# Attention with its row-maximum scores taken from the keys' high parts, two chunks at a time on two halves of TensorE's rows

## The chip, the cores and the metric

The kernel runs on one NeuronCore of a Trainium2 chip; the other cores are idle. The metric is the device time of one execution in microseconds. The engines have the profile's names: PE (TensorE's matmuls), PEld (its weight loads, which overlap with PE), DVE (VectorE), ACT (ScalarE), POOL (GpSimd) and SP (SyncE, which here only issues transfers). PSUM has eight banks of 2 KB for each of 128 partitions; a matmul writes to a bank, and DVE or ACT must read it before it can be used again.

## The reference

Attention for 4 batches and 12 heads of 448 tokens and 64 features, then two MLPs of 768 to 3072 to 768 features. All inputs and outputs are float32.

```python
def rmsnorm(x, g):
    rms = np.sqrt(np.mean(x * x, axis=-1, keepdims=True) + 1e-06)
    return x / rms * g
q_n, k_n = (rmsnorm(q, g_q), rmsnorm(k, g_k))
scores = scale * np.matmul(q_n, k_n.transpose(0, 1, 3, 2))
scores = scores - np.max(scores, axis=-1, keepdims=True)
attn = np.exp(scores)
attn = attn / (np.sum(attn, axis=-1, keepdims=True) + 1e-09)
return np.matmul(attn, v)
...
x = x + np.maximum(layernorm(x) @ w_ch1, 0.0) @ w_ch2
u = x + (token mixing of x by U and V, rank 32)
return u + np.maximum(u @ w_ch1, 0.0) @ w_ch2
```

The maximum that is subtracted appears in the numerator and in the sum under it. Another value near it gives the same quotient, apart from rounding.

## The kernel before

The kernel has two stages. Attention comes first, head by head, for 48 heads (up to about 345 us in the profile); the two MLPs follow, with an order of their own by a planner of costs and due times that the change does not touch. During attention some of the MLP weights are already loaded and prepared (`early`, `late`), and the layer norm of the batches that are done runs beside the heads (`ln_stats`, `ln_apply`).

Matrix products of float32 quality are made from float32r operands, which PE takes in one pass, with less precision. A value is split into a high part (its float32r rounding) and a low part (the rest). For each pair of heads `pre` makes from the raw inputs the token-wise tiles `qd` (the high part of q, written twice side by side), `kk` (high and low part of k side by side) and `ql` (the low part of q, and two columns more).

A head n then goes through these tasks, each written as a generator that is advanced once in each of the 4 steps of an iteration:

- `t1` (L419 to L437) turns `kk` and `qd` on PE so that features lie on partitions: `a1` [128, 448] has the high part of k on partitions 0 to 63 and the low part on 64 to 127, `bq` [128, 448] has the high part of q on both halves. ACT copies both from their banks (L427, L435).
- `mx` (L439 to L451) first copies the high part of k from `a1` into a second tile `a2` by a transfer on SP (L441). Then, for each of 4 chunks of 112 query tokens, one matmul (L445) gives the scores of the chunk with queries on partitions ("turned", since the later scores have keys there), and DVE takes each query's maximum from the bank (L446). ACT writes the negated maxima into a column of `ql` (L451).
- `t2` (L453 to L462) turns `ql`; its column with the maximum becomes a row that meets a row of ones in `a2`, so the later score matmul subtracts the maximum.
- `sc` (L464 to L486): for each of 4 chunks of 112 key tokens two matmuls into one bank, a 128-row one of `a1` and `bq` (L471) and a 66-row one of `a2` and the turned `ql` (L472); then ACT takes the exponential (L475).
- `pv` (L488 to L503): 4 products of exponentials and values (L496), float32, each issued as two instructions, accumulate in one bank `po`. The value tile `vf` has 128 columns: 64 of values, 64 filled with ones by POOL at the start (L260). So row 64 of `po` is the sum under the quotient.
- `norm` (L505 to L515): DVE copies rows 0 to 64 of `po` to `u` (two buffers), and SP stores them to `x` and to a table of sums (L513, L514).

The order around the change is written out by hand. `OS` is "smpabn": in iteration i the tasks are `sc` of head i, `mx` of head i + 2, `pv` of i - 1, `t1` of i + 3, `t2` of i + 1 and `norm` of i - 2, and each of the 4 steps advances each of them once in this order, after the background tasks (`pre`, `pre_v`). So PE gets in each step L471, L472, L445, L496, and at the end of the first three steps the turnings of k (L424), of `ql` (L459) and of q (L432). All engines run their instructions in order. The framework adds the waits, and lets the seven banks of this stage (`bank`, L61; an eighth serves the layer norm) go round among all these tasks.

Of the kernel before, what the change touches and what calls it, by code (L numbers as in the profile page):

```python
# [9 lines left out]
F32R = mybir.dt.float32r  # L10
# [4 lines left out]
ALU = mybir.AluOpType  # L15
AX = mybir.AxisListType

B, H, S, D = 4, 12, 448, 64
P = 128
CP = 112  # L20
NC = S // CP
# [14 lines left out]
QW = D + 2  # L36
# [7 lines left out]
def f32(ap):  # L44
    return ap.bitcast(F32)


def build(tc, qkv, gg, g_ln, w1a, w2a, w1b, w2b, u_in, v_in, out):
    nc = tc.nc
    V, A, PL, PE = nc.vector, nc.scalar, nc.gpsimd, nc.tensor  # L50
    with ExitStack() as es:
# [9 lines left out]
        def bank(name, tag=None):  # L61
            cnt[0] += 1
            tag = tag or banks["tag"]
            return banks["pool"].tile([P, 512], F32, tag=tag, name=f"{name}{cnt[0]}", bufs=banks[tag])
# [161 lines left out]
        def attention(ap, ep, ep2, early, late):  # L226
# [3 lines left out]
            st = {}  # L230
# [22 lines left out]
            for i in range(2):  # L253
                for lst, nm, dt, one in ((vfs, "vf", F32, 1.0), (vhs, "vh", F32R, 1.0), (vls, "vl", F32R, 0.0)):
                    n = NX if nm == "vf" else NC - NX
                    if n == 0:
                        lst.append(None)
                        continue
                    t = ap.tile([CP, 2, n, P], dt, tag=f"{nm}{i}", name=f"{nm}{i}")
                    PL.memset(f32(t[:, :, :, D:P]), one)  # L260
                    lst.append(t)
            for i in range(NA2):
                t = ap.tile([P, S], F32R, tag=f"a2{i}", name=f"a2{i}")
# [3 lines left out]
            for i in range(3):  # L267
                t = ep.tile([CP, 2 * NC, QW], F32R, tag=f"ql{i}", name=f"ql{i}")
# [150 lines left out]
            def t1(n):  # L419
                pr, j = divmod(n, 2)  # L420
                qd, ql, kk = st["tok", pr]
                pk = bank("pk")
                for c in range(NC):
                    PE.transpose(pk[:, c * CP:(c + 1) * CP].bitcast(F32R),  # L424
                                 kk[:, j * NC + c].rearrange("p a d -> p (a d)"), identr)
                a1 = ep2.tile([P, S], F32R, tag="a1", name=f"a1_{n}", bufs=T1 + 1)
                A.copy(a1, pk[:, :S])  # L427
                yield
                yield
                pq = bank("pq")  # L430
                for c in range(NC):
                    PE.transpose(pq[:, c * CP:(c + 1) * CP].bitcast(F32R),  # L432
                                 qd[:, j * NC + c].rearrange("p a d -> p (a d)"), identr)
                bq = ep2.tile([P, S], F32R, tag="bq", name=f"bq_{n}", bufs=T1 + 1)
                A.copy(bq, pq[:, :S])  # L435
                a2 = a2s[n % NA2]
                st["ab", n] = (a1, bq, a2)  # L437

            def mx(n):  # L439
                a1, bq, a2 = st["ab", n]  # L440
                nc.sync.dma_start(f32(a2[0:D, :]), f32(a1[0:D, :]))  # L441
                m = ap.tile([CP, NC], F32, tag="m", name=f"m{n}", bufs=2)
                for c in range(NC):
                    pm = bank("pm")
                    PE.matmul(pm[:CP, :S], bq[:, c * CP:(c + 1) * CP], a1, start=True, stop=True)  # L445
                    V.tensor_reduce(m[:, c:c + 1], pm[:CP, :S], AX.X, ALU.max)  # L446
                    if c < NC - 1:
                        yield
                pr, j = divmod(n, 2)
                ql = st["tok", pr][1]  # L450
                A.mul(ql[:, j * NC:(j + 1) * NC, D:D + 1], m.unsqueeze(2), -1.0)  # L451
# [36 lines left out]
            def pv(n):  # L488
                pr, j = divmod(n, 2)
                ps = st.pop(("p", n))  # L490
                vf, vh, vl = vfs[pr % 2], vhs[pr % 2], vls[pr % 2]
                po = bank("po")
                st["po", n] = po
                for c in range(NC):
                    if c < NX:
                        PE.matmul(po[:, :S], vf[:, j, c, :], ps[c], start=(c == 0), stop=(c == NC - 1))  # L496
                    else:
                        ph, pl = ps[c]
                        PE.matmul(po[:, :S], vh[:, j, c - NX, :], ph, start=(c == 0), stop=False)
                        PE.matmul(po[:, :S], vl[:, j, c - NX, :], ph, start=False, stop=False)  # L500
                        PE.matmul(po[:, :S], vh[:, j, c - NX, :], pl, start=False, stop=(c == NC - 1))
                    if c in PVY:
                        yield  # L503
# [55 lines left out]
            def ORD(i):  # L559
                fs = {"s": (sc, i), "m": (mx, i + MX), "p": (pv, i - 1), "a": (t1, i + T1), "b": (t2, i + T2), "n": (norm, i - NL)}  # L560
                return [fs[z] for z in OS]

            for i in range(-3 - T1, NH + 2):
                def ok(n):
                    return 0 <= n < NH
                if i == -3 - T1:
                    start = first_two()
# [40 lines left out]
        bufs, held, rings, ready = {}, {}, {}, {}  # L608
# [807 lines left out]
        with tc.tile_pool(name="raw", bufs=4) as rpool, tc.tile_pool(name="wf", bufs=3) as fpool:  # L1416
            with tc.tile_pool(name="ps", bufs=8, space=bass.MemoryType.PSUM) as psum:
                banks.update(pool=psum, tag="ps", ps=7, ln=1)
                with tc.tile_pool(name="att", bufs=1, side="right") as ap:
                    with tc.tile_pool(name="tok", bufs=1) as ep, tc.tile_pool(name="feat", bufs=1) as ep2:  # L1420
                        most, last = attention(ap, ep, ep2, early(), late())
# [70 lines left out]
```

## Time and profile before

| what | value |
|---|---|
| median of 3 runs (lowest to highest) | 1695.33 us (1694.02 to 1695.81) |
| profiled execution: span from its first to its last instruction | 1694.2 us |
| PE busy in the span | 1667.5 us (98%) |
| attention's matmuls | 11.6 to 345 us |
| the MLPs | from 345 us to the end |

Times in the rows further down are microseconds from the start of the span, unless they are marked as ns. A group of instructions has its line in the kernel, its engine, its operation, out <- in by the program's names, its shape and its count. A matmul's end is modelled and lies after the start of the next one, so durations of matmuls overlap; what one costs is read from the starts. A wait names the engine and line that ended it.

### The profile page before, as it was taken

The numbers are of one execution on the slowest core, as the hardware profiler recorded it, in microseconds if no ns is written. First come the engines' busy times: TensorE is split into PE (matmuls) and PEld (weight loads), VectorE is DVE, ScalarE is ACT, GpSimd is POOL, SyncE is SP. The second block draws the span as 40 slices with busy tenths as digits, with TensorE's granted clock in tenths as the row PEclk, the third lists the DMA queues.
The fourth block names the chain that finished last, engine by engine and source line by source line (L and its number), as shares of the span: only waits on it lengthen the run. The fifth ranks groups of instructions, "written<-read, shape, count | busy, mean of one in ns | idle before, by whom it ended". The sixth has DMA issues, their size and how long they took to land.

```text
span 1694.2 us, 24616 instructions
## 1 busy us (share of the span) xinstructions
PE 1667.5 (98%) x8223; PEld 1458.6 (86%) x8223; DVE 1198.0 (71%) x1913; ACT 997.2 (59%) x2098; POOL 1038.3 (61%) x924
## 2 busy tenths in 40 slices
PE   8999999999999999999999999999999999999999
PEld 6666666688898989999999999999999999999998
DVE  6767877878787876966767777666667864565665
ACT  6777878767777786554544455444445533544541
POOL 5445767457667777765555678545555645766752
PEclk8999999999999999999999999999999999999999
DMA  3434444775655576443544426565566563443442
GB/s 94 107 92 125 120 117 125 214 218 186 194 180 169 183 215 213 160 157 125 157 143 163 153 90 226 199 207 208 193 215 225 187 205 122 149 140 122 149 128 77
DMA packets 134430, 273.39 MB, mean 161 GB/s; under 512 B 37280, under 2 KB 57664, under 8 KB 134304
## 3 DMA queue, kind: packets, MB, share of 16 engines
q1 hardware_dynamic: 112252, 265.24, 49.4%
q10 hardware_dynamic: 22052, 6.59, 1.6%
q8 instruction: 65, 1.06, 0.3%
q14 instruction: 61, 0.50, 0.1%
HBM read 178.80 MB, written 81.96 MB: 154 GB/s over the span
## 4 chain that ended last, share of the span: by engine, by line
PE 85%; DVE 5%; DMA 4%; ACT 2%; issue 1%; POOL 1%; SPq 1%; DVEq 0%; ACTq 0%; POOLq 0%
PE bank L1104 31%; PE bank L1282 29%; PE po L496 6%; PE bank L1226 6%; PE b L1104 2%; PE ps L471 2%; PE pm L445 2%; PE b L1226 2%; PE ps L472 2%; DMA raw<-in_qkv 1%; DVE wf L83 1%; DMA r<-rs 1%; PE t L971 1%; PE xt L961 1%; PE pk L424 1%
## 5 line engine op out<-in xcount | busy, mean ns | idle before, releaser
L1282 PE MATMUL bank<-h,w 128*128 128x448 f32 x2655 | 588.6, 366 | 6.5 <-DVE x L1293 5.0
L1282 PEld LDWEIGHTS bank<-h,w 128*128 128x128 f32 x2655 | 497.0, 188 | 48.8 <-DVE x L1293 6.9
L1293 DVE TENSOR_TENSOR x<-x,bank 128x448 f32<-128x448 f32 x450 | 274.8, 615 | 182.1 <-PE bank L1282 177.8
L1104 PE MATMUL bank<-xh,w 128*128 128x448 f32 x1158 | 330.7, 367 | 0.0
L778 POOL TENSOR_TENSOR w<-wf,w 128x384 fp32r<-128x384 f32 x201 | 221.9, 1114 | 153.7 <-ACT w L777 143.8
L778 POOL TENSOR_TENSOR w<-s,w 128x384 fp32r<-128x384 f32 x151 | 171.8, 1141 | 161.5 <-ACT w L777 156.3
L1104 PE MATMUL bank<-T,w 128*128 128x448 f32 x1134 | 252.5, 367 | 2.9 <-DVE tm L1145 2.9
L1104 PEld LDWEIGHTS bank<-xh,w 128*128 128x128 f32 x1158 | 217.0, 188 | 18.3 <-issue 0.7
L1104 PEld LDWEIGHTS bank<-T,w 128*128 128x128 f32 x1134 | 211.7, 188 | 20.8 <-issue 2.7
L1104 PE MATMUL bank<-xl,w 128*128 128x448 f32 x579 | 211.9, 366 | 0.0
L777 ACT CAST w<-s 128x384 fp32r<-128x384 f32 x151 | 77.1, 514 | 171.9 <-PE bank L1104 164.0
L496 PE MATMUL po<-p,vf 112*128 112x448 f32 x384 | 176.1, 541 | 0.0
L777 ACT CAST w<-wf 128x384 fp32r<-128x384 f32 x201 | 102.4, 517 | 107.6 <-PE bank L1104 83.5
L446 DVE TENSOR_REDUCE m<-pm 112x1 f32<-112x448 f32 x192 | 118.5, 619 | 62.3 <-PE pm L445 61.6
L83 DVE SCALAR_TENSOR_TENSOR wf<-wf,raw 128x384 uint32<-128x384 uint32 x180 | 129.3, 724 | 23.0 <-ACT raw L75 10.1
L1104 PEld LDWEIGHTS bank<-xl,w 128*128 128x128 f32 x579 | 108.7, 188 | 8.9
L778 POOL TENSOR_TENSOR w<-raw,w 128x384 fp32r<-128x384 f32 x72 | 79.6, 1121 | 57.7 <-ACT w L777 57.7
L79 ACT ACTIVATE wf<-raw 128x384 f32<-128x384 f32 x180 | 99.4, 554 | 23.9 <-DMA raw<-in_w2a 14.5
L475 ACT ACTIVATE p<-ps 112x448 f32<-112x448 f32 x192 | 104.7, 546 | 3.2 <-PE pm L445 2.6
L71 ACT ACTIVATE raw<-raw 128x384 uint32<-128x384 uint8 x180 | 100.0, 557 | 0.0
L1096 DVE SCALAR_TENSOR_TENSOR h<-tm,h 128x448 fp32r<-128x448 f32 x103 | 97.1, 943 | 3.7 <-ACT h L1095 2.8
L471 PE MATMUL ps<-bq,a 128*112 128x448 f32 x192 | 98.7, 514 | 0.9 <-DVE m L446 0.9
(261 smaller groups left out, 2884.7 us busy)
## 6 DMA issues: line engine op xcount, KB each, us to landing
wd<-wf SPq DMA_DIRECT2D x94, 384.0 KB
ws<-w SPq DMA_DIRECT2D x84, 384.0 KB
w<-ws SPq DMA_DIRECT2D x84, 384.0 KB
wf<-wd SPq DMA_DIRECT2D x51, 384.0 KB
raw<-wd SPq DMA_DIRECT2D x48, 384.0 KB
raw<-in_w1b SPq DMA_DIRECT2D x48, 384.0 KB
raw<-in_w2b SPq DMA_DIRECT2D x48, 384.0 KB
raw<-in_w2a SPq DMA_DIRECT2D x44, 384.0 KB
```

Of the source, the lines that this page charges most:

```text
L71: A.activation(r[:, :, 0], r.bitcast(U8).rearrange("p n (t q) -> p n t q", t=2)[:, :, 0, 3], AF.Copy, scale=1.0 / 32, bias=-31.0 / 64)
L83: V.scalar_tensor_tensor(f, f, 3, r[:, :, 0], ALU.logical_shift_left, ALU.bitwise_or)
L446: V.tensor_reduce(m[:, c:c + 1], pm[:CP, :S], AX.X, ALU.max)
L471: PE.matmul(pb[:CP, :S], a1[:, cs], bq, start=True, stop=False)
L475: A.activation(p, pb[:CP, :S], AF.Exp)
L496: PE.matmul(po[:, :S], vf[:, j, c, :], ps[c], start=(c == 0), stop=(c == NC - 1))
L777: job(A, 520, lambda: A.copy(form(key)[0], src()), ins, ("hi",) + key, [key])
L778: job(PL, 1100, lambda: PL.tensor_tensor(form(key)[1], src(), f32(form(key)[0]), ALU.subtract), [("hi",) + key], key, rel=rel)
L1104: PE.matmul(out[:, :S], wt[:, k, :], xt[:, k, :], start=(first and n == 0), stop=(last and n == 8), skip_group_check=True)
L1226: PE.matmul(at(*to)[:, :S], wt[:, e, :], xt, start=(m in "13" and n == 0), stop=(n == 2), skip_group_check=True)
L1282: PE.matmul(at(*key)[:, :S], wt[:, e % 3, :], t, start=(n == 0), stop=(n == 3 * G - 1))
L1293: V.tensor_tensor(x[b][:, e, :], x[b][:, e, :], at(*key)[:, :S], ALU.add)
```

## The change

Three things are different.

- `t1` issues for every head but the first two one more transfer on SP, behind ACT's copy of `a1`: partitions 0 to 63 of `a1`, the high part of k, go to partitions 64 to 127 of a new tile `a3` (two buffers).
- `mx` takes for those heads, in the first and third of its four turns, two chunks at once: chunk c from rows 0 to 63 of `bq` and `a1`, chunk c + 1 from rows 64 to 127 of `bq` and `a3`, each a 64-row matmul into a bank of its own; DVE's two maxima follow. In the second and fourth turn it issues nothing. The scores for the maximum are now high part of q by high part of k alone; the term with the low part of k is left out of them. The scores for the exponentials are as before.
- The value tile `vf` has QW = 66 columns instead of 128, so L496 writes 66 rows of its bank.

```diff
-                    t = ap.tile([CP, 2, n, P], dt, tag=f"{nm}{i}", name=f"{nm}{i}")
-                    PL.memset(f32(t[:, :, :, D:P]), one)
+                    t = ap.tile([CP, 2, n, QW], dt, tag=f"{nm}{i}", name=f"{nm}{i}")
+                    PL.memset(f32(t[:, :, :, D:QW]), one)
...
                 a1 = ep2.tile([P, S], F32R, tag="a1", name=f"a1_{n}", bufs=T1 + 1)
                 A.copy(a1, pk[:, :S])
+                if n > 1:
+                    st["a3", n] = a3 = ap.tile([P, S], F32R, tag="a3", name=f"a3_{n}", bufs=2)
+                    nc.sync.dma_start(f32(a3[D:P, :]), f32(a1[0:D, :]))
...
+                a3 = st.pop(("a3", n), None)
                 for c in range(NC):
-                    pm = bank("pm")
-                    PE.matmul(pm[:CP, :S], bq[:, c * CP:(c + 1) * CP], a1, start=True, stop=True)
-                    V.tensor_reduce(m[:, c:c + 1], pm[:CP, :S], AX.X, ALU.max)
+                    if a3 is None:
+                        pm = bank("pm")
+                        PE.matmul(pm[:CP, :S], bq[:, c * CP:(c + 1) * CP], a1, start=True, stop=True)
+                        V.tensor_reduce(m[:, c:c + 1], pm[:CP, :S], AX.X, ALU.max)
+                    elif c % 2 == 0:
+                        pms = [bank("pm") for _ in range(2)]
+                        for pm, kt, z, h in zip(pms, (a1, a3), (c, c + 1), (slice(0, D), slice(D, P))):
+                            PE.matmul(pm[:CP, :S], bq[h, z * CP:(z + 1) * CP], kt[h], start=True, stop=True)
+                        for z, pm in enumerate(pms):
+                            V.tensor_reduce(m[:, c + z:c + z + 1], pm[:CP, :S], AX.X, ALU.max)
                     if c < NC - 1:
                         yield
...
-                        PE.matmul(po[:, :S], vf[:, j, c, :], ps[c], start=(c == 0), stop=(c == NC - 1))
+                        PE.matmul(po[:QW, :S], vf[:, j, c, :], ps[c], start=(c == 0), stop=(c == NC - 1))
```

## Rows read from the trace of the kernel before

**Rows 1.** The page's first part: busy time, share and instructions of each engine.

```profile
PE 1667.5 (98%) x8223; PEld 1458.6 (86%) x8223; DVE 1198.0 (71%) x1913; ACT 997.2 (59%) x2098; POOL 1038.3 (61%) x924
```

**Rows 2.** Windows: stretch, length, busy us (instructions) of each engine, granted clock, DMA share, GB/s.

```profile
60.00:331.00 271.00, 265.66 (x1294) 180.98 (x1294) 206.78 (x381) 216.21 (x511) 164.04 (x139) 1.00 0.48 126
331.00:345.00 14.00, 14.00 (x51) 8.42 (x49) 10.89 (x23) 11.71 (x30) 2.86 (x4) 1.00 0.67 206
345.00:1694.00 1349.00, 1336.07 (x6607) 1229.68 (x6605) 942.21 (x1430) 727.54 (x1462) 843.48 (x748) 1.00 0.52 171
```

**Rows 3.** PE's longest waits, 60 to 350 us: us in total, times, longest.

```profile
PE pm L445 <- ACT bq L435: 2.2, 4, 0.8
PE pt L459 <- ACT wf L79: 1.3, 1, 1.3
PE ps L471 <- DVE m L446: 0.9, 1, 0.9
```

**Rows 4.** PE's longest wait after 350 us.

```profile
PE bank L1282 <- DVE x L1293: 5.0, 5, 1.5
```

**Rows 5.** Timeline of PE, two steps of attention's end: start, us, instruction.

```profile
330.20 0.71 PE L471 MATMUL ps<-bq,a 128*112 128x448 f32 x1
330.75 0.37 PE L472 MATMUL ps<-t,a 66*112 66x448 f32 x1
330.96 0.37 PE L445 MATMUL pm<-a,bq 128*112 128x448 f32 x1
331.16 0.92 PE L496 MATMUL po<-p,vf 112*128 112x448 f32 x2
331.57 0.72 PE L471 MATMUL ps<-bq,a 128*112 128x448 f32 x1
332.12 0.37 PE L472 MATMUL ps<-t,a 66*112 66x448 f32 x1
332.33 0.92 PE L496 MATMUL po<-p,vf 112*128 112x448 f32 x2
332.73 0.71 PE L471 MATMUL ps<-bq,a 128*112 128x448 f32 x1
```

**Rows 6.** Timeline of PE, products of the last heads in one run.

```profile
341.48 3.92 PE L496 MATMUL po<-p,vf 112*128 112x448 f32 x10
```

**Rows 7.** Groups by form, weight loads, 0 to 500 us: busy, mean ns, idle before.

```profile
L496 PEld LDWEIGHTS po<-p,vf 112*128 112x128 f32 x384 | 73.5, 192 | 9.4 <-issue 1.1 <-DVE m L446 0.2 <-ACT wr L71 0.2
L445 PEld LDWEIGHTS pm<-a,bq 128*112 128x112 f32 x192 | 34.4, 179 | 16.1 <-ACT bq L435 10.0 <-issue 1.0
L459 PEld LDWEIGHTS pt<-identr,ql 112*66 112x66 f32 x192 | 16.5, 114 | 23.2 <-issue 16.8 <-ACT wf L79 2.0 <-ACT a L427 1.9
```

**Rows 8.** Timeline of PEld, three loads of 128 columns in a row.

```profile
158.20 0.31 PEld L424 LDWEIGHTS pk<-identr,kk 112*128 112x128 f32 x3 [0.24 <-issue]
```

**Rows 9.** The start: POOL's fills (ns min/median/max), and a wait of PE's.

```profile
L260 POOL MEMSET vf<- x2: 524/526/528, 0.9 to 1.7; 112x512 f32 x2
...
28.35 0.46 PE L445 MATMUL pm<-a,bq 128*112 128x448 f32 x1 [1.64 <-ACT bq L435]
```

**Rows 10.** Timeline around 165 us: SP's transfers, ACT's copy of a1, the next head's scores.

```profile
162.55 0.46 SPq L441 DMA_DIRECT2D a<-a  x1
...
165.13 0.53 ACT L427 CAST a<-pk 128x448 fp32r<-128x448 f32 x1
...
165.33 0.89 SPq L240 DMA_DIRECT2D raw<-in_qkv  x2
...
170.13 0.37 PE L445 MATMUL pm<-a,bq 128*112 128x448 f32 x1
```

**Rows 11.** DMA, 162 to 172 us in 40 slices: busy tenths, GB/s.

```profile
DMA  0000002960000396053389999998610039500000
GB/s 0 0 0 0 0 0 57 251 144 7 0 0 0 79 237 143 10 118 89 56 258 374 400 337 293 267 212 169 149 29 0 0 93 229 136 0 0 0 0 0
```

**Rows 12.** DVE's longest wait, 60 to 331 us.

```profile
DVE m L446 <- PE pm L445: 50.7, 61, 1.9
```

## The prediction, before any run of the changed kernel

> **What bounds the kernel now.** I read the page first: TensorE (PE) is busy for 98% of the span, the other engines for 59 to 71% [rows 1]. An average says nothing of a stage, so the windows come next. Attention's steady part, 60 to 331 us, has PE busy for 265.7 of 271 us at a granted clock of 1.00 (the 2.4 GHz level), ACT for 216.2 (80%), DVE for 206.8 (76%); its tail to 345 has PE busy throughout; the two MLPs have 1336 of 1349 [rows 2]. Then the waits: between 60 and 350 us PE's largest are 2.2, 1.3 and 0.9 us in total [rows 3], after 350 the largest is 5.0 us [rows 4]. So PE is the bound before and after the edit, and a microsecond taken from PE in attention should bring everything behind it forward.
>
> What one turned-score matmul (L445) costs on PE is read from where they run out. With one in it a step runs from 330.20 to 331.57, 1.37 us; the next step, without it, from 331.57 to 332.73, 1.16 us [rows 5]. The price is 0.21 us; the spacing of the starts around it agrees, 330.75 to 330.96 to 331.16. The 0.37 us of its record are no price, since the next matmul starts 0.2 us after it.
>
> **The change part by part.**
>
> *Two matmuls at once.* Heads 2 to 47 take it (n > 1): 46 heads with 2 pairs each, 92 pairs, and 184 matmuls of 128 rows become 184 of 64 rows, two on separate halves of the array. No matmul of the trace uses half of the rows, so I bound it. Good end: the second costs nothing, and 92 x 0.205 = 18.9 us go. Other end of a pair without a mode cost: both run one after the other, 0. In between stands the loading of weights. A load of 112 columns takes 0.179 us [rows 7], and a load behind another one follows it after about 0.104 us (three in 0.31 us, 128 columns) [rows 8]. If the pair's loads can start only when the matmul ahead has taken its own weights, the second half is ready after 0.179 + 0.104 = 0.28 us and not after 0.205: 0.075 us are exposed. I take half of that, 0.04, since some of the second load may lie beside the first: a pair then costs 0.245 in place of 0.41 us and saves 0.165; 92 x 0.165 = **15.2 us**.
>
> The Trainium skill ("TensorE: Matmul & The Clock Gate", Measured speedup vs the span model) gives about 4 ns for each further tile of a pack; by that the sum would be 18.5 us, near the good end. No run here shows it yet.
>
> *The copy a3.* Each of the 46 heads issues one more transfer of 112 KB on SP, a1's upper half (its high parts) moved to the lower partitions. SP has to wait for ACT's copy of a1; what stands behind it are the stores of the head before (x and its sums) and the loads of raw inputs. A sample: a1's copy runs from 165.13 to 165.66; the issue itself takes 0.46 us; the like copy a2, issued at 162.55, shows its traffic in four slices of 0.25 us that end at 164.5, about 1.95 us from its issue [rows 10, 11]. So a3 lands near 167.6. Its reader is the next head's first pair, now at 170.13 [rows 10]: 2.5 us to spare, 2.2 with a head some 0.33 us shorter. The stores that are now about 1.8 us later have two buffers, so a head's time of room. Nothing on the path: 0, with the late copy as a rival.
>
> *Two maxima together.* The DVE reads both banks one after the other in every other step. DVE waited 50.7 us for these matmuls in the stretch [rows 12], so it has room. One of the seven banks is held some 0.6 us longer; PE's wait for DVE's maximum is 0.9 us now [rows 3]. I take 0, at worst some tenths in a few heads.
>
> *The narrower value tile.* Weights of 66 instead of 128 columns load in about 0.114 instead of 0.192 us [rows 7]. They lie behind matmuls: each of the two instructions of a product takes 0.375 us, (3.92 - 0.54) / 9, in the run of ten [rows 6], and the first one's load lies beside L445 (0.205 us) or, now, the pair. I take 0; the other end is that this load sets the 0.02 us between 0.205 and the 0.187 of half a product's instruction, 192 x 0.018 = 3.5 us. The filled columns were never read. The two fills on POOL (0.53 us each, done by 2.2 us) get shorter [rows 9]; what PE waits for early is ACT (1.64 us at 28.35) [rows 9], so 0.
>
> *What is given back.* At the start, heads 2 and 3 stand beside such waits: their 4 pairs, 0.7 us, count as lost. Behind that ACT rises from 80% to 216.2 / 257 = 84% of a shorter stretch and will be late in a few more places; I put 0.9 us, a fifth of the 4.4 us of waits seen [rows 3].
>
> **The sum.** 15.2 - 0.7 - 0.9 = 13.6 us. The profiled span is 1694.2 us, the median of the runs 1695.3, so 1.1 us lie around the span: 1694.2 - 13.6 + 1.1 = 1681.7. Forecast **1681.5 us**; its own range, from 18.9 plus some of the 3.5 us to a saving of 10, is 1675 to 1685.
>
> **Rivals.**
>
> *The array empties at each change between whole and halves (ends slower).* Its place is before and behind each pair. A matmul's record is 0.37 us long where its successor starts after 0.205: 0.165 us of it are passage through the array [rows 5]. If a pair must wait for that and the product (L496) again, a pair costs 0.205 + 2 x 0.165 = 0.535 us in place of 0.41: 92 x 0.125 = 11.5 us slower, 1706.8. It decides once the two waits together cost more than 0.205 us, 0.10 each. For it: nothing in the trace could have shown it. Against it: between 128 rows (L471), 66 rows (L472) and 128 again nothing is lost at the second change (0.21 us, 330.75 to 330.96) [rows 5]; but none of these splits the array. If in addition no weights could be loaded ahead, 0.18 and 0.19 us more stand open at each pair [rows 7], 92 x 0.49 = 45 us, 1740; that is the outer end.
>
> The Trainium skill states this rule ("TensorEngine Tiling (Array Packing)", Key Properties): a change of the tiling mode, not of the tile alone, drains TensorE. By it the time is the rival's 1706.8; the trace neither agrees nor disagrees.
>
> *The halves don't run side by side.* If the second's weights wait until the first matmul has begun, a pair takes two matmuls' time as now: 1695, no change. For it: every load in the trace is issued one ahead of its matmul, no more. Against it: the loads in question go to different rows.
>
> *The copy comes late.* Loads of raw inputs, issued at 165.33, fill the DMA engines from 166.25 to about 169.25 [rows 10, 11]. If a3 goes behind them it lands near 169.8, and its reader then comes at 170.13 - 0.33: break-even. Where a store or a load more lies before it, up to 0.6 us are lost in every second head; on a mean of half of that, 23 x 0.3 = 7 us: 1688.5, still faster. For it: one such load per two heads, DMA shares of 0.48 and, at the end, 0.67 [rows 2]. Against it: a3 stands ahead of those loads in program order.
>
> **Chances.** Forecast as reasoned (pairs overlap, little given back) 0.47; late copy 0.11; one after the other 0.13; emptying array at the rival's size 0.24; its outer end 0.05. The first two are faster by over 0.2%, which is 3.4 us and about what a measurement can tell from no change: 0.58. Within: 0.13. Slower: 0.29. The sign turns on a price that no row shows, so the range has to reach over it: from 1675 up to 1708, just past the rival's 1706.8; left out are the outer end and half a tenth at the edges.
>
> **What would show it.** Right: in a steady head the two L445-like matmuls of a pair start within 0.1 us of each other; from the second's start to the product about 0.2 us; a step with a pair lasts some 0.03 to 0.04 us longer than 1.37 us, the step after it 1.16; the last turned score falls near 317 instead of 331; MLP windows the same length. Emptying: 0.35 us and more from L472 to the pair and from the pair to the product. One after the other: starts 0.2 us apart. Late copy: PE waits named after a DMA of a at the pair's second half, in every second head. The prediction is wrong if attention's end doesn't move earlier by about 14 us, or if it does and the MLPs give it back by waits on DMA or DVE.

## The result and the profile after

The changed kernel takes 1710.49 us (median of 4 runs, 1708.45 to 1714.47) where the one before took 1695.57 us beside it: ratio 1.0093, 95% interval 1.0080 to 1.0106. It is slower by 0.9%, and lies 2.5 us outside the predicted range. The profiled execution took 1708.45 us with a span of 1706.7 us, 12.5 us more than the span before.

The page's first part and the clock of its 40 slices, as in [rows 1]: PE has 16.6 us more of busy time with the same number of instructions, its weight loads 39 us less.

```profile
PE 1684.1 (99%) x8223; PEld 1419.7 (83%) x8223; DVE 1195.0 (70%) x1913; ACT 999.3 (59%) x2098; POOL 1043.8 (61%) x924
...
PEclk7999999999999999999999999999999999999999
```

The windows of the changed kernel, as in [rows 2]: attention's steady part and the MLPs. The first MLP matmul starts at 354.98 us instead of 344.89; so attention lost 10.1 us of the 12.5, and the MLPs 2.4 (1349.3 us before, 1351.7 after).

```profile
60.00:344.00 284.00, 281.01 (x1311) 147.66 (x1309) 205.28 (x387) 220.58 (x518) 168.81 (x140) 0.99 0.53 137
358.00:1707.00 1349.00, 1334.78 (x6593) 1228.32 (x6591) 942.16 (x1430) 726.85 (x1460) 845.82 (x748) 1.00 0.52 170
```

The timeline of PE over a step without and a step with a pair (L455 is the pair, L482 and L483 the scores, L507 the product), to be held against [rows 5]:

```profile
168.61 0.44 PE L482 MATMUL ps<-bq,a 128*112 128x448 f32 x1
168.89 0.37 PE L483 MATMUL ps<-t,a 66*112 66x448 f32 x1
169.09 0.92 PE L507 MATMUL po<-p,vf 112*66 112x448 f32 x2
169.50 0.72 PE L470 MATMUL pt<-identr,ql 112*66 112x112 f32 x4
170.06 0.42 PE L482 MATMUL ps<-bq,a 128*112 128x448 f32 x1
170.32 0.37 PE L483 MATMUL ps<-t,a 66*112 66x448 f32 x1
170.62 0.46 PE L455 MATMUL pm<-a,bq 64*112 64x448 f32 x2
171.00 0.97 PE L507 MATMUL po<-p,vf 112*66 112x448 f32 x2
171.46 0.79 PE L435 MATMUL pq<-identr,qd 112*128 112x112 f32 x4
```

Without a pair the step runs from 168.61 to the turning at 169.50, 0.89 us; with one from 170.06 to 171.46, 1.40 us. A pair costs 0.51 us where two whole matmuls cost 0.41. The spacing shows where: L483 to the pair 0.30 instead of 0.205, the pair to the product 0.38, the product to what follows 0.46 instead of 0.41. The weight loads of the same pair, behind the load of one L445 in the kernel before (first fence), say what happens there:

```profile
330.75 0.18 PEld L445 LDWEIGHTS pm<-a,bq 128*112 128x112 f32 x1
```

```profile
170.62 0.17 PEld L455 LDWEIGHTS pm<-a,bq 64*112 64x112 f32 x2 [0.33 <-DVE sy L149]
...
171.00 0.20 PEld L507 LDWEIGHTS po<-p,vf 112*66 112x66 f32 x2 [0.21 <-issue]
```

Both loads of the pair are done in 0.17 us, the time of one, so the halves are loaded beside each other. But ahead of them PEld is idle for 0.33 us, and again for 0.21 us ahead of the product's: a load that the kernel before issued one matmul early (330.75, its matmul at 330.96 [rows 5]) is held until the change. (The engine named as the releaser is not what it waited for; it is only what ended last.) Little else holds PE. Its waits between 60 and 362 us are fewer than in [rows 3]:

```profile
PE pm L455 <- DVE x L562: 1.8, 1, 1.8
PE pm L455 <- ACT bq L438: 0.6, 2, 0.4
PE ps L482 <- DVE u L521: 0.2, 1, 0.2
```

From head to head this gives, between the turnings of k, 6.68 us in place of 6.45 (heads 12 to 14: 86.01, 92.70, 99.36 us; before 84.07, 90.52, 96.97): 0.23 us a head, 0.11 a pair.

One piece is no matter of pairs' spacing. Head 4 turns its keys at 30.75 us instead of 29.05, and the granted clock of the start differs. Stretches of 5 us, kernel before, then changed kernel:

```profile
20.00:25.00 5.00, 5.00 (x29) 4.12 (x29) 3.31 (x8) 4.28 (x12) 2.48 (x3) 0.67 0.10 23
25.00:30.00 5.00, 3.37 (x20) 2.37 (x19) 3.08 (x7) 4.49 (x12) 5.00 (x5) 1.00 0.39 115
30.00:35.00 5.00, 5.00 (x20) 3.33 (x19) 2.98 (x7) 2.28 (x6) 2.10 (x3) 0.66 0.21 49
```

```profile
20.00:25.00 5.00, 5.00 (x24) 3.51 (x23) 3.46 (x8) 3.45 (x10) 2.19 (x3) 0.50 0.20 46
25.00:30.00 5.00, 4.93 (x19) 2.77 (x18) 2.36 (x6) 4.28 (x10) 5.00 (x5) 0.50 0.19 44
30.00:35.00 5.00, 5.00 (x18) 2.53 (x18) 2.89 (x7) 2.60 (x8) 2.06 (x3) 0.64 0.38 83
```

Both fall to the lower level (1.2 GHz, 0.50) after PE has waited 2.9 us for the keys of head 2 at 16 to 19 us. Before, the clock is back within the first stretch and falls once more, for a short time, after a wait at 27 us; with pairs on halves from head 2 on it stays low until about 33 us.

The 10.1 us that attention lost are a balance. Up to the first MLP matmul PE is busy for 15.0 us more and waits 4.9 us less than before (kernel before, then changed kernel):

```profile
0.00:344.89 344.89, 331.33 (x1618) 228.81 (x1619) 255.76 (x483) 269.56 (x637) 194.75 (x177) 0.99 0.48 125
```

```profile
0.00:354.98 354.98, 346.33 (x1619) 188.73 (x1619) 250.71 (x481) 270.61 (x634) 196.99 (x176) 0.97 0.52 136
```

### The profile page after: what moved, and what is told of

It reads as the page before. It is cut to its first block, busy times and chain, and to the rows that moved or that the text cites. A ratio compares the mean times of both kernels' runs of the same rounds, so it can differ in the third digit from the quotient of the medians.

```text
span 1706.7 us, 24733 instructions
## 1 busy us (share of the span) xinstructions
PE 1684.1 (99%) x8223; PEld 1419.7 (83%) x8223; DVE 1195.0 (70%) x1913; ACT 999.3 (59%) x2098; POOL 1043.8 (61%) x924
## 4 chain that ended last, share of the span: by engine, by line
PE 80%; DVE 6%; DMA 4%; POOL 3%; ACT 3%; issue 2%; SPq 1%; ACTq 0%; DVEq 0%; POOLq 0%
PE bank L1115 28%; PE bank L1293 27%; PE po L507 7%; PE bank L1237 6%; PE b L1115 2%; PE ps L482 2%; PE b L1237 2%; PE pm L455 2%; POOL w L789 2%; PE ps L483 2%; DVE wf L83 1%; DMA raw<-in_qkv 1%; POOL s L864 1%; DMA r<-rs 1%; DVE x L1304 1%
## 5 line engine op out<-in xcount | busy, mean ns | idle before, releaser
L507 PE MATMUL po<-p,vf 112*66 112x448 f32 x384 | 182.0, 557 | 0.2
L457 DVE TENSOR_REDUCE m<-pm 112x1 f32<-112x448 f32 x184 | 107.0, 618 | 48.8 <-PE pm L455 48.0
L482 PE MATMUL ps<-bq,a 128*112 128x448 f32 x192 | 100.1, 521 | 0.2 <-DVE u L521 0.2
```

The source lines that it names most:

```text
L457: V.tensor_reduce(m[:, c + z:c + z + 1], pm[:CP, :S], AX.X, ALU.max)
L482: PE.matmul(pb[:CP, :S], a1[:, cs], bq, start=True, stop=False)
L507: PE.matmul(po[:QW, :S], vf[:, j, c, :], ps[c], start=(c == 0), stop=(c == NC - 1))
```

## The experiments

Theory A was the prediction's first rival: every change between whole rows and halves empties the array. Against it stood B (what was lost lies beside PE: copies, two maxima at once, banks) and C (the halves themselves are slow, or run one behind the other).

**The price by itself.** Blocks of matmuls with constant operands ahead of the first head:

```diff
+            for _ in range(24):
+                mm(wa, full)
+            for _ in range(24):
+                mm(wa, up)
+                mm(wb, low)
+            for _ in range(24):
+                mm(wa, full)
+                mm(wa, up)
+                mm(wb, low)
...
```

> Six blocks of matmuls of 448 columns stand ahead of the first head; each is read by the spacing of its starts. Theory A (a change between whole rows and halves empties the array on both sides, and the halves of a pair run side by side): whole rows 0.205 us each; pairs alone 0.205 us a pair; whole + pair in turn about 0.72 us a unit (0.205 + 0.52); whole + one upper half in turn about the same 0.7 us; upper halves alone 0.205 us each; two whole + two pairs about 1.13 us a unit (2 x 0.205 + 0.72). Rival C (no cost of a change; the halves are slow or run one behind the other): pairs alone 0.5 us a pair, whole + pair 0.72, whole + upper half 0.46, upper halves alone 0.26, two + two pairs 1.45. Rival B (what was lost lies beside PE): pairs 0.205, whole + pair 0.41, whole + upper half 0.41, two + two 0.82. The total time says nothing here.

The timeline of PE in the second and the third block (wa and wb are the two banks; a row of two in the third block is a whole matmul and the upper half behind it):

```profile
16.05 0.36 PE L258 MATMUL wa<-xh 64*112 64x448 f32 x1
16.07 0.36 PE L258 MATMUL wb<-xh 64*112 64x448 f32 x1
...
21.92 0.84 PE L258 MATMUL wa<-xh 128*112 128x448 f32 x2
22.31 0.46 PE L258 MATMUL wb<-xh 64*112 64x448 f32 x1
22.69 0.84 PE L258 MATMUL wa<-xh 128*112 128x448 f32 x2
```

Pairs alone start every 0.20 us, the two halves 0.01 to 0.02 us apart: they do run side by side, at the rate of one whole matmul. Whole and pair in turn take 0.77 us a unit (20.37 to 38.11 us for 23 of them) where 0.40 would do without a price. Each change costs 0.37 / 2 = 0.185 us, in either direction (0.39 us from whole to half, 0.38 back). Two whole and two pairs in turn took 1.19 us a unit, again 0.39 above 0.80. C falls; A holds with a price somewhat above what I had expected of it (0.72 and 1.13). What the rows show is the price, and loads that don't run ahead; that the array is empty in between is A's reading of it.

The fourth and fifth block (whole and one upper half in turn; upper halves alone) brought something else. Stretches with the granted clock in the third column from the end: pairs alone, whole and pair in turn, then the fourth block, which begins at 38.88 us, upper halves alone (64.9 to 74.5) and the last block:

```profile
15.40:20.30 4.90, 4.90 (x49) 4.30 (x48) 2.37 (x5) 2.72 (x4) 3.74 (x3) 1.00 0.00 0
20.37:38.88 18.51, 18.51 (x74) 8.28 (x72) 0.00 (x0) 0.00 (x0) 0.03 (x1) 1.00 0.00 1
38.88:46.00 7.12, 7.12 (x20) 3.20 (x18) 0.00 (x0) 0.00 (x0) 0.00 (x0) 0.94 0.00 0
70.00:75.00 5.00, 5.00 (x14) 3.68 (x13) 0.00 (x0) 0.00 (x0) 0.00 (x0) 0.50 0.00 0
80.00:90.70 10.70, 10.70 (x56) 4.89 (x54) 0.00 (x0) 0.00 (x0) 0.00 (x0) 1.00 0.01 2
```

PE counts as busy all the time, yet with single halves in it the clock falls to the lower level and stays there; in the last block, two whole and two pairs, it is back.

**What counts as a change, and how long a run must be.** The second set of blocks:

```diff
+            for _ in range(16):
+                mm(wa, 0, P)
+                mm(wb, 0, QW)
...
+            for _ in range(6):
+                for _ in range(4):
+                    mm(wa, 0, P)
+                for _ in range(4):
+                    mm(wa, 0, D)
+                    mm(wb, D, P)
```

> Blocks of matmuls of 448 columns ahead of the first head, read by the spacing of starts. What counts as a change: 16 whole rows; 16 times whole and 66 rows; 16 times whole and 96 rows; 6 times 4 whole and 4 pairs of halves. Theory A (only the split into halves counts, and a run of halves pays one entry and one exit, whatever its length): whole with 66 rows and whole with 96 rows 0.40 us a unit; 4 whole + 4 pairs 8 x 0.20 + 0.37 = 1.97 us a unit, so four pairs in a run cost 1.17 us where eight whole matmuls cost 1.60. Rival (any other number of rows costs something, or each pair behind a first one too): 0.5 us and more a unit for the first two, 2.4 us for the last. The total time says nothing here.

```profile
14.30 0.37 PE L258 MATMUL wb<-xh 66*112 66x448 f32 x1
14.50 0.37 PE L258 MATMUL wa<-xh 128*112 128x448 f32 x1
...
28.22 0.46 PE L258 MATMUL wb<-xh 64*112 64x448 f32 x1
...
29.22 1.45 PE L258 MATMUL wa<-xh 128*112 128x448 f32 x5
30.22 0.46 PE L258 MATMUL wb<-xh 64*112 64x448 f32 x1
```

Whole with 66 rows takes 0.41 us a unit, and so does whole with 96 rows: no price. Four whole and four pairs take 2.00 us a unit (28.22 to 30.22), 0.37 above 4 x 0.207 + 4 x 0.20: one entry and one exit, whatever the length of the run.

The Trainium skill ("TensorEngine Tiling (Array Packing)", Key Properties) has the rule without a size: a change of mode drains TensorE, a change of the tile alone does not. These runs agree: 0.185 us for a change, nothing between the tiles of a pair.

**The same order without halves.**

```diff
-                            PE.matmul(pm[:CP, :S], bq[h, z * CP:(z + 1) * CP], kt[h], start=True, stop=True)
+                            PE.matmul(pm[:CP, :S], bq[:, z * CP:(z + 1) * CP], a1, start=True, stop=True)
```

> The changed kernel with its order, its copies a3 and its narrow value tile, but all four turned-score matmuls with all 128 rows of a1 and bq (a3 is filled and not read). Theory A: the loss is gone, 1692 to 1698 us. Rival B (copies on SP, two maxima together, banks): stays near 1710. Rival C: also gone.

1695.90 us against 1695.37 before: ratio 1.0005 (0.9996 to 1.0014). The copies, the two maxima at once, the order and the narrow value tile cost nothing that can be measured (a head takes 6.44 us where nothing waits, 6.45 before); B falls. But its attention ended at 340.90 us, 4.0 us sooner than before, and the span is only 0.5 us shorter. That opened the second question below.

**One run of two pairs per head.**

```diff
-                    elif c % 2 == 0:
+                    elif c == 0:
                         pms = [bank("pm") for _ in range(2)]
-                        for pm, kt, z, h in zip(pms, (a1, a3), (c, c + 1), (slice(0, D), slice(D, P))):
+                        for z in range(NC):
+                            pm, kt, h = pms[z % 2], (a1, a3)[z % 2], (slice(0, D), slice(D, P))[z % 2]
```

> Both pairs of a head behind each other in the first of the four steps, the second pair into the same two banks; DVE takes the maxima of the last two chunks only and copies them for the first two (so half of the maxima are another chunk's). Theory A: one entry and one exit per head in place of two, 46 x 0.31 = 14 us less than the changed kernel, and 46 x (0.82 - 0.72) = 4.6 us less than before: about 1691 to 1696 us. Rival C: the pairs cost what they cost, 1706 to 1711. Rival B: two DVE maxima fewer per head, otherwise 1705 to 1711.

1702.49 us, ratio 1.0049 (1.0028 to 1.0069): 8 us less than the changed kernel, as A has it in direction, but not below before. Where nothing waits a head takes 6.36 us (90.79 to 97.15), 0.09 less than before. It waits, though: the run needs all of a3 and bq at the head's first step. PE's largest waits up to 360 us:

```profile
PE pm L456 <- ACT bq L438: 4.5, 5, 1.2
PE pm L456 <- DMA a<-a: 3.7, 7, 1.3
```

This is the late copy of the prediction's third rival, in a kernel with shorter heads and an earlier reader. Together with a start as slow as the changed kernel's (head 4 at 31.45 us) attention ends 2.7 us later than before, and the MLPs take 3.0 us longer.

**The run two steps later, in four banks.** From head 4 on, all maxima taken from their own chunks.

```diff
-                    elif c % 2 == 0:
-                        pms = [bank("pm") for _ in range(2)]
+                    elif c == 2:
+                        pms = [bank("pm") for _ in range(NC)]
```

> All four chunks of a head from head 4 on in one run of two pairs in the third of the four steps, each in a bank of its own, with all its maxima; the copy a3 and bq have two steps more to arrive. Theory A (one entry and one exit, 0.74 us a head in place of 0.82): the waits for a3 and bq that the run in the first step had (8 us) are gone, 44 x 0.08 = 3.5 us less than before in attention: 1691 to 1696 us in all. Rival G (four banks at once are too many of seven): PE waits for DVE's maxima or for transposes' banks, 0.2 us and more per head, 1700 us and more.

1705.19 us, ratio 1.0065 (1.0050 to 1.0080): rival G by the time. The waits for a3 are gone, and in 27 of the 44 heads the run stays whole (first row below); such a head takes 6.35 us where nothing waits, 0.10 less than before, as A has it. In 13 heads the fourth matmul comes behind the product, as a run of its own with an entry and an exit of its own, and such a head takes 6.9 us where nothing else waits; in the other 4, PE waits for 0.5 to 1.1 us within the run until ACT or DVE has read a bank:

```profile
97.62 0.66 PE L456 MATMUL pm<-a,bq 64*112 64x448 f32 x4
...
165.32 0.66 PE L456 MATMUL pm<-a,bq 64*112 64x448 f32 x3
165.91 0.97 PE L508 MATMUL po<-p,vf 112*66 112x448 f32 x2
166.80 0.45 PE L456 MATMUL pm<-a,bq 64*112 64x448 f32 x1
167.18 0.97 PE L508 MATMUL po<-p,vf 112*66 112x448 f32 x2
```

That the fourth matmul comes late for want of a free bank in the 13 heads too is likely and not shown: its place there is set by the order in which the program was built.

**One half alone.** The kernel before, each turned-score matmul on rows 0 to 63 only.

```diff
-                    PE.matmul(pm[:CP, :S], bq[:, c * CP:(c + 1) * CP], a1, start=True, stop=True)
+                    h = slice(0, D if n > 1 else P)
+                    PE.matmul(pm[:CP, :S], bq[h, c * CP:(c + 1) * CP], a1[h], start=True, stop=True)
```

> The kernel before with each turned-score matmul of heads 2 to 47 taking only rows 0 to 63 of bq and a1 (the high parts), one per step, no copies a3 and no pairs. Theory A: each of 184 matmuls costs an entry and an exit and saves nothing, 184 x 0.31 = 57 us slower than before, about 1752. Rival C: 184 x 0.05 = 9 us, about 1705. Rival B: as before, 1693 to 1698.

1871.67 us (one execution), far beyond every expectation. Two of its windows tell why (the granted clock stands third from the end); attention lasts until 521 us here:

```profile
280.00:300.00 20.00, 20.00 (x52) 9.75 (x51) 6.30 (x11) 7.65 (x18) 3.63 (x5) 0.59 0.19 47
340.00:400.00 60.00, 60.00 (x241) 31.19 (x242) 39.95 (x74) 41.36 (x96) 29.79 (x26) 1.00 0.45 124
```

From 20 us to nearly 300 the clock stood at the lower level (0.50 as the mean of 20 to 100 us), then it came back, with the same single halves in every step, and stayed at 1.00. So the total says nothing on the price, but the second part does: at 1.00 a head takes 7.92 us (342.12 to 365.87 us for three) in place of 6.45, and each of its four matmuls 1.47 / 4 = 0.37 us more than a whole one. That is theory A with the price of the blocks, for halves that save nothing; C's 0.05 and B's 0 are out.

**The start.** The changed kernel with pairs from head 4 on.

```diff
-                if n > 1:
+                if n > 3:
```

> The changed kernel, but the pairs on halves only from head 4 on (n > 3). Theory F (at the start the pairs of heads 2 and 3 hold the clock at its lower level until 33 us, which makes the 1.7 us that head 4 is late there): clock back at 1.00 by about 24 us, as before, and 1.5 to 2.5 us less than the changed kernel, 1707 to 1709. Rival: the clock stays low as long, and the time is that of the changed kernel less 4 x 0.1 us.

1705.08 us, ratio 1.0061 (1.0044 to 1.0078). The clock of 20 to 30 us is that of the kernel before (0.67, then 1.00), and head 4 comes at 29.20 us instead of 30.75. So theory F is right on the place. The medians differ by 5.4 us, more than the 1.6 us there and the four pairs' 0.4 us; the two intervals are 2 to 3 us wide to either side. The profiled executions differ by 3.2 us: the MLPs begin 1.1 us sooner (353.84 against 354.98) and take 2.1 us less. In attention part of the gain is lost again, since here PE does wait for the copy a3, 1.9 us in all. What the rest of the 5.4 us is stays open.

**What a saving is worth.** The kernel before without the turned-score matmuls of chunks 1 and 3.

```diff
-                    pm = bank("pm")
-                    PE.matmul(pm[:CP, :S], bq[:, c * CP:(c + 1) * CP], a1, start=True, stop=True)
-                    V.tensor_reduce(m[:, c:c + 1], pm[:CP, :S], AX.X, ALU.max)
+                    if n < 2 or c % 2 == 0:
+                        pm = bank("pm")
+                        PE.matmul(pm[:CP, :S], bq[:, c * CP:(c + 1) * CP], a1, start=True, stop=True)
+                        for z in range(1 if n < 2 else 2):
+                            V.tensor_reduce(m[:, c + z:c + z + 1], pm[:CP, :S], AX.X, ALU.max)
```

> The kernel before, but heads 2 to 47 leave out the turned-score matmuls of chunks 1 and 3 (92 matmuls of 128 rows); DVE takes both maxima from the bank of the chunk ahead, so half of the maxima are another chunk's. This is what the change would have brought if a pair cost what one matmul costs. Theory D (PE time taken from attention comes off the end): 92 x 0.205 = 18.9 us, 1676 to 1679 us. Rival E (the MLPs start with work that isn't ready sooner, as in the run with full rows, where attention ended 4.0 us sooner and the span only 0.5): attention ends 17 to 19 us sooner, the MLPs take 5 to 12 us longer, 1682 to 1691 us.

1689.42 us against 1695.43, ratio 0.9967 (0.9955 to 0.9978): 6 us, not 18.9. Attention ends at 330.19 us, 14.7 sooner; the MLPs then take 1359.2 instead of 1349.3 us of the span. Most of the loss sits in the first 40 us of the MLPs. The second 20 us behind attention, kernel before, then this one:

```profile
365.00:385.00 20.00, 18.10 (x88) 16.10 (x87) 19.39 (x26) 16.23 (x30) 10.29 (x9) 1.00 0.60 192
```

```profile
348.00:368.00 20.00, 13.43 (x48) 10.92 (x47) 13.19 (x16) 14.33 (x29) 12.22 (x10) 0.81 0.62 198
```

PE, DVE, ACT and POOL are each idle for about a third of this stretch. The chain of waits there names what they had waited for: weights for the MLPs' first step, which come in, are put together, go out to memory and come back.

```profile
330.56 6.59 DMA wr<-in_w1a
...
341.85 3.10 DMA wd<-wf
...
345.82 6.22 DMA wf<-wd
```

The waits are the smaller part of it. Over the whole of the MLPs PE runs the same 6607 instructions, but is busy for 1342.4 us in place of 1336.2 (kernel before, then this one):

```profile
344.89:1694.20 1349.31, 1336.18 (x6607) 1229.80 (x6605) 942.21 (x1430) 727.65 (x1462) 843.59 (x748) 1.00 0.52 171
```

```profile
330.19:1689.40 1359.21, 1342.42 (x6607) 1234.26 (x6605) 948.27 (x1441) 730.16 (x1472) 848.16 (x749) 0.99 0.51 171
```

So 6.2 of the 9.9 us are matmuls that take longer, and 3.7 us more waiting. They take longer because the granted clock is at its lower level behind the waits (by windows of 1 us that gives about 6 us); the longest wait and the stretch that follows it:

```profile
354.36 5.97 PE L1284 MATMUL bank<-h,w 128*128 128x448 f32 x15 [3.03 <-ACT h L1097]
```

```profile
354.00:360.00 6.00, 5.64 (x15) 4.96 (x16) 5.19 (x6) 5.18 (x12) 6.00 (x6) 0.50 0.45 135
```

And the opposite, 92 matmuls added to the kernel before:

```diff
-                    PE.matmul(pm[:CP, :S], bq[:, c * CP:(c + 1) * CP], a1, start=True, stop=True)
+                    for _ in range(2 if n > 1 and c % 2 == 0 else 1):
+                        PE.matmul(pm[:CP, :S], bq[:, c * CP:(c + 1) * CP], a1, start=True, stop=True)
```

> The kernel before with the matmuls of chunks 0 and 2 of heads 2 to 47 done twice into the same bank: 92 matmuls more, 92 x 0.205 = 18.9 us of PE in attention. Theory E (before stands at the point where PE's work and the transfers for the MLPs' first step are ready together: what is taken from attention comes off the end by a third, what is added comes on in full): 1712 to 1716 us. Rival H (the MLPs' start takes up what is added too, as it gave back what was taken): 6 to 10 us, 1701 to 1706.

1712.46 us against 1694.48, ratio 1.0092 (1.0071 to 1.0113), 18.0 us for 18.9 us of matmuls; attention ends 19.1 us later and the MLPs take 1349.7 us of the span, as before. So theory E: attention's PE work and these transfers are ready at about the same time. What is added comes on at the end in full, what is taken comes off only by a third. That the transfers are what sets the other side is read from the chain; no kernel with fewer of them was tried.

## Why the prediction was wrong

**What bounds the kernel** was right for a loss and wrong for a gain. PE is the bound in attention, but "a microsecond taken from PE in attention should bring everything behind it forward" fails: of 14.7 us only 4.8 us of the span were left. The term "what is given back" was put at 1.6 us, the start included; in the run with 18.9 us of matmuls left out it measured 4.2 us in attention (18.9 less 14.7) and 9.9 behind it, 3.7 of waits and 6.2 of the lower clock behind them. The rows I read could not tell: PE's waits [rows 3, 4] say that the transfers were not late yet, and not how soon they would be.

**The pair** is the step that failed first: its cost was put at 0.245 us, and in the kernel it is 0.51. I took 0.245 us from between the two ends, by an argument on the weight loads. The loads turned out to lie beside each other, the halves start 0.01 us apart, and the good end would have been right for a pair among pairs (0.20 us). The Trainium skill ("TensorE: Matmul & The Clock Gate", Measured speedup vs the span model) gives about 4 ns for each further tile. Pairs alone show 0.01 to 0.02 us here, more than that but next to nothing. What I left out of the forecast was the price of entering and leaving, which I had only as a rival. Its size, from the 0.165 us by which a record outlasts the spacing, was 0.535 us for a pair; measured are 0.51 in the kernel and 0.57 in the blocks (0.77 - 0.20). The sign was decided by two changes costing more than 0.205 us together; they cost 0.31 and 0.37 (and 0.37 each with a single half).

My argument against it, that 128 and 66 rows follow each other for nothing, was a true observation about something else: beside whole rows, 66 and 96 rows have no price (0.41 us for two). Of the row counts tried, only the halves have one.

**The rival's time**, 1706.8, is 1.7 us below the profiled run (1708.45) and 3.7 below the median. That attention lost 10.1 us, where 92 x 0.10 to 0.12 is 9 to 11, is in part luck. PE was busy for 15.0 us more. Besides the pairs these hold some 5 us of lower clock, which no case held (an estimate: by windows of 1 us PE works about 10 us longer at 0.50 than before, at 20 to 33 us and, behind the wait of 1.8 us, at 313 to 317). The 4.9 us that PE waited less make up for them. The MLPs' 2.4 us come on top. The kernel with pairs from head 4 on lies 5.4 us lower, inside the range; how much of that is the clock stays open.

**The side terms** were right. The copy a3 was never waited for in the changed kernel, the two maxima cost one wait of 1.8 us (behind a DVE instruction that itself waited for a transfer), the narrow value tile nothing: together ratio 1.0005. The late copy is real where its reader comes earlier (3.7 us in the one-run kernel), and 1.9 us of it show in the kernel with pairs from head 4 on. "One after the other" is excluded.

## What to carry to other kernels

Packing small matmuls on parts of the array pays by the run, not by the pair: with 0.37 us for entering and leaving and 0.205 us saved per pair, one pair between whole matmuls loses, two together gain 0.1 us at most, and only longer runs win more, if banks and operands are there for them. Before a saving in one stage is carried to the end of the sum, look at what must be ready where the next stage starts: a kernel whose PE and transfers meet there pays a loss in full and gives back most of a gain, here, behind attention, more by the clock that was low behind the waits than by the waits. A cheap probe is to add work and to leave work out, and to see whether both move the end alike.

## What the runs showed of the hardware that was not expected

- A change between whole rows and halves costs 0.185 us each way in the blocks, at a granted clock of 1.00 (2.4 GHz) with 448 columns (0.31 us for both ways in the kernel), and no weights are loaded ahead across it (PEld idle 0.21 to 0.33 us); between whole, 96 and 66 rows there is no such price.
- A busy PE did not always have its clock. With one half in use alone the granted clock fell from 1.00 to 0.50 in the blocks and stayed there from about 45 to 79 us; in the kernel with single halves it was low from 20 to nearly 300 us and then 1.00 for the 220 us behind, with the same work. Pairs alone, and whole matmuls and pairs in turn, kept 1.00; pairs in the first heads, after the clock had fallen in a wait, kept it low until 33 us. What decides it these runs don't tell; the kernel with single halves and the blocks were each executed once.
